# First batch of an attention and MLP kernel: inputs laid out as six tokens a row, and one order for its softmax and weight conversions

## The chip, the cores and the metric

One core of a Trainium2 chip. The metric is the device time of one execution in microseconds (us), median of several. TensorE (PE) multiplies matrices; VectorE (DVE), ScalarE (ACT) and GpSimd (POOL) work elementwise; the SP queue issues the DMA transfers.

## What is computed

Inputs q, k, v are (8 batches, 8 heads, 576 tokens, 64), phi is (8, 8, 576, 32). The first stage, cut:

```
a = exp(phi - max over tokens); a = a / sum over tokens
k_m, v_m = einsum('bhsm,bhsd->bhmd', a, k or v)         # 32 memory rows a head
attn = softmax(q @ k_m.T / 8)
x = (attn @ v_m), heads side by side: (8, 576, 512)
xn = (x - mean) / sqrt(var + 1e-6) * g_ln
x = x + relu(xn @ w_ch1) @ w_ch2                          # 512 -> 2048 -> 512
```

A second block follows (gelu, a token-mixing matrix, w_out), which the change does not touch. w_ch1 and w_ch2 come as 64-bit floats, read as pairs of 32-bit words.

## The kernel before, in words

Phase 1 (`phase1`) does attention and the first MLP for batch after batch, phase 2 the second block. Matrix products run in a split form: each operand is a high part and a low remainder, three products together.

*The first batch.* `load_phi`, `load_kv`, `load_rem` (L180 to L216) lay 512 of the 576 tokens as four consecutive tokens on each of 128 partitions, and the other 64 (REM) in tiles of their own (`prz`, `kvr`). `prep_max` and `prep_exp` (L246 to L278) take the maximum over tokens and the exponential, `prep_sum` (L280) adds up on POOL, `prep_kv` (L304) multiplies phi with keys and values into `kvp`, `prep_norm` scales to `kvn`, `prep_T` turns it to `kvT`. Queries: `load_q` and `t_q` (L363) bring five tiles of 128 tokens (the last 64) and turn them; `t_scores` (L388) forms scores `sc` in three groups of tiles (0 and 1, 2 and 3, 4), turns them (`z`), takes the maximum (L413), subtracts it (L414) and exponentiates (L415); `t_norm` (L418) divides by the sum; `t_attn` (L426) turns back and splits into `aTh`, `aTl`.

*The weights.* w_ch1 comes in four quarters (fb 0 to 3) of four 128-row blocks (`load_w1`, 4 KB rows). `to_f32` (L105) turns the 64-bit words: one ScalarE step on the upper words (L114) and two VectorE steps (L115, L116). `scale_w1` (L493) multiplies by g_ln on ScalarE (L499), `center_w1` (L501) forms column means on TensorE (`cm`, L505) and subtracts them on VectorE (L507). `make_vw` (L518) multiplies with `kvT` (`pvw`, L545), and `evict_vw` (L549) splits the result into `vw`. So the MLP's first product needs only `aT` and `vw`. w_ch2 comes in 16 blocks: `split_w2` (L558) converts each and splits it (L128 on ScalarE, L129 on POOL).

*The MLP.* `m1` (L582) forms a block `ph` (L593) with `aT` and `vw`, 256 or 320 tokens wide, in two banks by turns, and `relu` evicts it (`hh` on ScalarE L579, `hl` on VectorE L580). `m2` (L612) multiplies with `w_ch2`, three blocks later. Batch 0 goes by quarters: both token ranges with fb 0 (256 wide, then 320), then both with fb 1, and so on.

*What sets the order.* Every step is an event with a written-out time (`at_time`); events run in order of time and give instructions their priority, and a planner then places them on each engine's queue by when it expects their inputs. `tc.issue_after(x)` keeps an instruction behind x in that order. All loads go out on one queue (SP). Raw weights and several other tiles share a pool of 19 buffers (`wpool`), so a load can wait for a buffer.

Of the kernel before, what the change touches and what calls it, by code (L numbers as in the profile page):

```python
# [28 lines left out]
def fused_kernel(ctx: ExitStack, tc: tile.TileContext, q, k, v, phi, g1, w1, w2, w_in, g2, w_sg, b_sg, w_out, out):  # L29
# [45 lines left out]
    es_mlp, es_w2, es_attn, es_right, es_left = ExitStack(), ExitStack(), ExitStack(), ExitStack(), ExitStack()  # L75
# [28 lines left out]

    def to_f32(raw, gate=None):  # L105

        words = raw.bitcast(U32).rearrange("p (n two) -> p n two", two=2)
        lo, hi = words[:, :, 0], words[:, :, 1]

        gates = ExitStack()  # L110
        for ins in gate or ():
            gates.enter_context(tc.issue_after(ins.ins))
        with gates:
            A.activation(hi.bitcast(F32), hi.bitcast(F32), AF.Prelu, scale=2.0 ** -112, alpha=-(2.0 ** 32))  # L114
            V.tensor_scalar(lo, lo, 29, None, op0=ALU.logical_shift_right)  # L115
            V.scalar_tensor_tensor(out=lo, in0=hi, scalar=3, in1=lo, op0=ALU.logical_shift_left, op1=ALU.bitwise_or)  # L116
        return lo.bitcast(F32)

    def split(raws, wp, scale=None, gate=None):
# [3 lines left out]
        for i, raw in enumerate(raws):  # L123
# [3 lines left out]
            if scale is None:  # L127
                A.copy(h, w)  # L128
# [16 lines left out]
    def phase1():  # L145
# [8 lines left out]
        tail = pool(es_w2, "tail", 1)  # L154
# [8 lines left out]
        st = {"lays": [], "ps0": 0}  # L163

# [14 lines left out]

        def load_phi(b, gs):  # L180
# [47 lines left out]
        def load_q(u, b, i):  # L228
            n = u["n"]
            if b == 0:  # L230
                if i % 2 == 0:
                    t = wpool.tile([P, 2, DM], F32, tag="w", name="q0") if i == 4 else tail.tile([P, 2, DM], F32, tag="vw", name="q0", bufs=VTAIL)
                    st["q0"] = t[:, 0, :], t[:, 1, :]
                t = st["q0"][i % 2].rearrange("p (c o d) -> p c o d", c=4, o=2)[:n]
                load(t.rearrange("p c o d -> p (c o) d"), q[b, :, i * P:i * P + n, :].rearrange("h p d -> p h d"))
# [68 lines left out]
        def prep_kv(b, gs):  # L304
# [3 lines left out]
            lands = [n for t in (*(t for g in gs for t in ts[g]), st["kvr", b]) for n in t[1]] if b else []  # L308
# [16 lines left out]
            for g in gs:  # L325
                if b == 0:
                    st["kvp", g] = kvps[:, g]
                else:
                    prep_norm(b, g, kvps[:, g])

        def prep_norm(b, g, kvp=None):
# [3 lines left out]
            V.tensor_scalar(kvn[:, :, g, :], st["kvp", g] if kvp is None else kvp, rs[:, g:g + 1], None, op0=ALU.mult)  # L335

        def prep_vb(b):
            kvn = st["kvn", b]
            VBh, VBl = VBs[b % 2]
            with tc.issue_after(st["kvT", b][1].ins):  # L340
# [7 lines left out]
        def prep_T(b):  # L348
# [5 lines left out]
            st["kvT", b] = kvT, A.copy(kvT, pt)  # L354
# [8 lines left out]
        def t_q(gr, i):  # L363
# [9 lines left out]
            if b == 0:  # L373
                pt = ps_0([P, 4, n], "ptq")
                for c in range(4):
                    PE.transpose(pt[:, c, :], t[:, c].rearrange("p o d -> p (o d)"), ident[:n, :n])
                A.copy(out, pt)
# [10 lines left out]
        def t_scores(gr):  # L388
# [5 lines left out]
            sc = [ps_of(b, [P, w], "sc") for _ in range(2)]  # L394
            claims = [V.memset(t[:, 0:2], 0.0).ins.name for t in sc] if b else []
            with whole(b):
                for kT, cs in parts:
                    for j in range(4):
                        for g in range(2):
                            rs_, ms = slice(64 * g, 64 * g + 64), slice(32 * j, 32 * j + 32)  # L400
                            mm = PE.matmul(sc[g][ms, cs], kT[rs_, ms], qT[rs_, j, cs], start=True, stop=True, skip_group_check=True)
                            for name in claims:
                                tc.add_manual_dep(mm.ins, name, ORDER, reason="all eight parts of the array together")
            nb = 2 * w // 32
# [4 lines left out]
            for g in range(2):  # L409
                V.transpose(out=z[:, g * w:(g + 1) * w], in_=sc[g])  # L410
# [713 lines left out]
```

## Time and profile before

| | us |
|---|---|
| three runs | 1202.42, 1204.23, 1206.3 |
| median | 1204.23 |
| the profiled execution | 1205.68 |
| its span | 1203.5 |

Over the span TensorE is busy 97%, VectorE 57%, ScalarE 39%, POOL 33%, and the mean granted clock is 0.988. In the lines below, times count from the span's start; a bracket at the end of an instruction's line is the time its engine stood idle before it and what ended that. [...]

### The profile page before, as it was taken

The numbers are of one execution on the slowest core, as the hardware profiler recorded it, in microseconds if no ns is written. First come the engines' busy times: TensorE is split into PE (matmuls) and PEld (weight loads), VectorE is DVE, ScalarE is ACT, GpSimd is POOL, SyncE is SP. The second block draws the span as 40 slices with busy tenths as digits, with TensorE's granted clock in tenths as the row PEclk, the third lists the DMA queues.
The fourth block names the chain that finished last, engine by engine and source line by source line (L and its number), as shares of the span: only waits on it lengthen the run. The fifth ranks groups of instructions, "written<-read, shape, count | busy, mean of one in ns | idle before, by whom it ended". The sixth has DMA issues, their size and how long they took to land.

```text
span 1203.5 us, 20688 instructions
## 1 busy us (share of the span) xinstructions
PE 1170.4 (97%) x7711; PEld 993.1 (83%) x7711; DVE 688.0 (57%) x1669; ACT 467.7 (39%) x1071; POOL 401.8 (33%) x622
## 2 busy tenths in 40 slices
PE   4899899999999999999999999999999999999998
PEld 3486678788788888788888888889989988998997
DVE  4886665755644645644546445567476377447532
ACT  3665332323332322422333445445444354344430
POOL 2234112311201211201211112456666475566641
PEclk9799899999999999999999999999999999999999
DMA  8984834463341543231410343032240052022201
GB/s 248 354 242 120 236 80 126 93 194 76 97 117 31 146 124 67 92 108 25 126 35 27 108 125 116 27 82 88 82 139 18 19 150 69 2 84 84 79 19 71
DMA packets 198900, 124.14 MB, mean 103 GB/s; under 512 B 93072, under 2 KB 174096, under 8 KB 198800
## 3 DMA queue, kind: packets, MB, share of 16 engines
q1 hardware_dynamic: 198800, 122.82, 35.4%
q8 instruction: 61, 1.00, 0.3%
q14 instruction: 39, 0.32, 0.1%
HBM read 99.72 MB, written 31.33 MB: 109 GB/s over the span
## 4 chain that ended last, share of the span: by engine, by line
PE 88%; DVE 6%; DMA 2%; SPq 1%; ACT 1%; issue 1%; POOL 1%; POOLq 0%; ACTq 0%; DVEq 0%
PE ph L593 16%; PE py L623 10%; PE py L625 10%; PE py L624 10%; PE pvs L1029 9%; PE po L1052 8%; PE pv L920 8%; PE pu L1004 7%; PE pvw L545 3%; DMA q<-q_d 1%; PE kvp L315 1%; SPq L87 1%; PE cm L505 1%; PE px L460 1%; DVE qT L379 1%; PE px L459 1%
## 5 line engine op out<-in xcount | busy, mean ns | idle before, releaser
L593 PE MATMUL ph<-aTh,vw 128*128 128x320 f32 (+1 forms) x1024 | 248.4, 301 | 1.4 <-ACT vw L551 1.4
L623 PE MATMUL py<-whl,hh 128*128 128x512 f32 x512 | 202.3, 397 | 6.7 <-ACT hh L579 6.5
L624 PE MATMUL py<-whl,hh 128*128 128x512 f32 x512 | 201.2, 393 | 0.0
L593 PEld LDWEIGHTS ph<-aTh,vw 128*128 128x128 f32 x1024 | 179.5, 191 | 26.0 <-issue 8.8
L625 PE MATMUL py<-whl,hl 128*128 128x512 f32 x512 | 182.7, 397 | 0.0
L579 ACT ACTIVATE hh<-ph 128x256 fp32r<-128x256 f32 x256 | 96.5, 386 | 168.5 <-PE ph L593 111.0
L580 DVE SCALAR_TENSOR_TENSOR hl<-ph,hh 128x256 fp32r<-128x256 f32 x256 | 106.4, 421 | 91.1 <-ACT hh L579 90.6
L593 PE MATMUL ph<-aTl,vw 128*128 128x256 f32 (+1 forms) x512 | 152.7, 299 | 0.0
L623 PEld LDWEIGHTS py<-whl,hh 128*128 128x128 f32 x512 | 96.5, 189 | 30.1 <-ACT hh L579 8.6
L1029 PE MATMUL pvs<-wsh,vhl 128*128 128x288 f32 x576 | 121.1, 295 | 0.0
L624 PEld LDWEIGHTS py<-whl,hh 128*128 128x128 f32 x512 | 96.7, 189 | 19.0 <-issue 0.5
L1004 PE MATMUL pu<-yTh,whl 128*128 128x288 f32 x512 | 111.0, 296 | 0.2 <-DVE ug L909 0.2
L593 PEld LDWEIGHTS ph<-aTl,vw 128*128 128x128 f32 x512 | 97.7, 191 | 11.2 <-issue 3.6
L625 PEld LDWEIGHTS py<-whl,hl 128*128 128x128 f32 x512 | 90.3, 190 | 11.9 <-issue 2.3
L1029 PEld LDWEIGHTS pvs<-wsh,vhl 128*128 128x128 f32 x576 | 94.4, 189 | 0.7
L920 PE MATMUL pv<-whl,yTh 128*128 128x512 f32 x288 | 91.0, 396 | 0.0
L1052 PE MATMUL po<-whl,gh 128*128 128x512 f32 x288 | 90.1, 391 | 0.0
L1004 PEld LDWEIGHTS pu<-yTh,whl 128*128 128x128 f32 x512 | 85.4, 189 | 1.9 <-DVE ug L909 0.9
L579 ACT ACTIVATE cr<-ph 128x64 fp32r<-128x64 f32 x128 | 28.7, 226 | 126.3 <-PE ph L593 125.7
L1032 POOL TENSOR_TENSOR gt<-gt,ug 128x288 f32<-128x288 f32 x64 | 52.9, 827 | 68.3 <-DVE gt L1031 61.8
L1029 PE MATMUL pvs<-wsl,vhl 128*128 128x288 f32 x256 | 75.6, 295 | 0.0
L1004 PE MATMUL pu<-yTl,whl 128*128 128x288 f32 x256 | 75.5, 295 | 0.0
(154 smaller groups left out, 2164.5 us busy)
## 6 DMA issues: line engine op xcount, KB each, us to landing
raw<-in_moe_w_ch_dram SPq DMA_DIRECT2D x32, 512.0 KB, 7.8
wc<-w_d SPq DMA_DIRECT2D x28, 512.0 KB, 5.7
y_d<-x SPq DMA_DIRECT2D x36, 256.0 KB, 2.2
yt<-y_d SPq DMA_DIRECT2D x36, 256.0 KB, 2.7
yr<-y_d SPq DMA_DIRECT2D x36, 256.0 KB, 2.8
kv<-in_k_dram SPq DMA_DIRECT2D x32, 256.0 KB, 3.9
kv<-in_v_dram SPq DMA_DIRECT2D x32, 256.0 KB, 4.0
out_dram<-yr SPq DMA_DIRECT2D x32, 256.0 KB, 2.0
```

The costliest lines, as they stand in the source:

```text
L545: mm = PE.matmul(ps[g][ms, :], vT[rs_, ms], ws[j // 2][rs_, j % 2, :], start=True, stop=True, skip_group_check=True)
L579: high = A.activation(out_h, src, AF.Relu)
L580: return high, V.scalar_tensor_tensor(out=out_l, in0=src, scalar=0.0, in1=out_h.bitcast(F32), op0=ALU.max, op1=ALU.subtract)
L593: R["ph"] = PE.matmul(ph, w_[:, ks], x[:, g, 0:w], start=(n == 0), stop=(n == 3 * HK - 1))
L623: PE.matmul(py, hh, wh, start=start, stop=False)
L624: PE.matmul(py, hh, wl, start=False, stop=False)
L625: PE.matmul(py, hl, wh, start=False, stop=stop)
L920: PE.matmul(pv, y[:, kc, cs], w, start=(n == 0), stop=(n == 3 * KC - 1))
L1004: PE.matmul(pu, w[:, ds_], y[:, kc, cs], start=(n == 0), stop=(n == 3 * KC - 1))
L1029: PE.matmul(pvs, v_, w_, start=(n == 0), stop=(n == len(ops) - 1))
L1032: G.tensor_tensor(out=gt, in0=gt, in1=ug, op=ALU.mult)
L1052: PE.matmul(po, gg[:, dc, cs], w, start=(n == 0), stop=(n == 3 * KC - 1))
```

## The change

For the first batch alone, phi, keys and values are loaded as six consecutive tokens on each of 96 partitions (no leftover tiles), queries of tiles 0 to 3 as pairs of consecutive tokens on 128 partitions. Sums over tokens are matmuls with a column instead of POOL additions. These inputs lie in a pool of their own (`start`), whose memory goes to the `tail` pool afterwards. The order of loads becomes: phi, keys and values, first query pair, W1 blocks 0 and 1, second query pair, W1 blocks 2 and 3, last query tile, W2 blocks 0 to 3, then fb 1; W2 blocks 4 and 5 come ahead of fb 2. On VectorE and ScalarE the first batch's conversions and softmax steps are each kept behind the one before (`st["v"]`, `st["act"]`), W2 blocks 1 to 3 behind the softmax of the last group, and fb 1 behind these. The scores of the last group take banks of another pool. Later batches keep their steps. Cut to its core:

```diff
+    def behind(gate):
+        es = ExitStack()
+        for ins in gate or ():
+            es.enter_context(tc.issue_after(ins.ins))
+        return es
...
+        def load_first(g):
+            load(st["phi", 0][:P0, 4 * g:4 * g + 4], phi[0, g].rearrange("h (p c) m -> p h c m", c=C0))
+        def load_kv0(g, n):
+            t = start.tile([P, 2, 2, C0, D], F32, name=f"kv0{g}{n}")
+            for i, src in enumerate((k, v)):
+                load(t[:P0, i], src[0, g, 2 * n:2 * n + 2].rearrange("h (p c) d -> p h c d", c=C0))
...
+        def kv_first(g):
+            for c in range(C0):
+                PE.matmul(st["sums"][:, g:g + 1], w, mcol[:P0], start=(c == 0), stop=(c == C0 - 1), skip_group_check=True)
+            for c in range(C0):
+                for j in range(4):
+                    PE.matmul(
+                        st["kvp", 0][32 * j:32 * j + 32, g],
+                        ex[:, c, j, :],
+                        st["kv0", g, j // 2][:P0, :, j % 2, c, :],
...
+        def norm_first():
+            with behind([R["word"]]):
+                V.tensor_scalar(rs, st["sums"], float(DM), 1e-9, op0=ALU.mult, op1=ALU.add)
...
         def t_q(gr, i):
...
-                    PE.transpose(pt[:, c, :], t[:, c].rearrange("p o d -> p (o d)"), ident[:n, :n])
+                            for o in range(2):
+                                PE.matmul(pt[64 * o:64 * o + 64, c, :], t[:, 2 * c + o], ident, start=True, stop=True, skip_group_check=True)
...
+        def scale_w1(fb, part=range(KC)):
...
+                    w = to_f32(raws[fb][j], [st["hl"], R["word"]] if "hl" in st else [first_grs[2]["ah"], st["v"], R["word"]])
...
         def split_w2(c):
...
-            gate = st.get("hl", tiles[1 if c == 0 else 3]["tr"])
-            W2[c] = split([raws.pop(("w2", c))], wpool, gate=[gate])
+            W2[c] = split([raws.pop(("w2", c))], wpool, gate=[st["hl"]] if c > 3 else [st["v"], st["act"]])
+            if c < 4:
+                st["v"], st["act"] = R["word"], R["high"]
...
-                        at_time(-27, load_q, us[i], ub, qi)
-                        at_time(-21 + 0.1 * tt, t_q, gr, i)
+                        at_time((-27, -26.7, -26.5)[gi], load_q, us[i], ub, qi)
+                        at_time((-20, -18.04, -17.5)[gi] + 0.01 * i, t_q, gr, i)
...
-                    at_time(-17 + 0.1 * tt, t_scores, gr)
-                    at_time(-16 + 0.1 * tt, t_norm, gr)
-                    at_time(-16 + 0.1 * tt, t_attn, gr)
+                    at_time((-18.05, -17.93, -16.35)[gi], t_scores, gr)
+                    at_time((-18.0, -17.92, -16.34)[gi], t_soft, gr)
+                    at_time((-17.3, -16.3, -16.1)[gi], t_norm, gr)
+                    at_time((-17.2, -16.2, -16.0)[gi], t_attn, gr)
...
+            if fb == 0:
+                at_time(-26.8, load_w1, 0, [0, 1])
+                at_time(-26.6, load_w1, 0, [2, 3])
+                for j in range(KC):
+                    at_time((-20.2, -19.5, -18.08, -18.02)[j], pre_w1, j)
+                    at_time((-20.1, -19.0, -18.07, -17.95)[j], word_w1, j)
+                    at_time((-18.09, -18.06, -18.01, -17.94)[j], scale_w1, 0, [j])
+            else:
+                at_time((-25.7, -2.5, 2.0)[fb - 1], load_w1, fb, range(KC))
+                at_time((-5.0, 3.0, 7.5)[fb - 1], scale_w1, fb)
+            at_time((-17.9, -0.3, 3.0 + 1.6, 7.5 + 1.6)[fb], center_w1, fb)
+            at_time((-17.1, 1.3, 3.0 + 2.8, 7.5 + 2.8)[fb], make_vw, 0, [fb])
...
-            split_at = 4.5 * (c // 4) + 0.5625 * (c % 4) - 0.6 if c > 3 else 0.9 * c - 4
-            at_time(split_at - 5 if c > 3 else -12.7 if c == 3 else 0.2 * c - 26.4, load_w2, c)
+            split_at = 4.5 * (c // 4) + 0.5625 * (c % 4) - 0.6 if c > 3 else (-17.0, -15.9, -15.8, -15.7)[c]
+            at_time(split_at - 5 if c > 5 else 0.1 * c - 3.2 if c > 3 else 0.2 * c - 26.4, load_w2, c)
```

`pre_w1` is the ScalarE step of `to_f32`, `word_w1` its two VectorE steps, `t_soft` the part of `t_scores` from the turning of the scores on.

## Rows read from the trace of the kernel before

**Rows 1.** Busy time by stretch: PE, PEld, DVE, ACT, POOL, clock, DMA share, GB/s.
```profile
0.00:13.00 13.00, 2.33 (x9) 1.39 (x9) 5.09 (x11) 1.98 (x3) 2.88 (x13) 1.00 0.70 196
13.00:24.00 11.00, 9.88 (x136) 6.84 (x136) 1.72 (x7) 4.91 (x13) 4.89 (x9) 1.00 0.96 247
24.00:41.50 17.50, 11.16 (x40) 3.03 (x40) 16.91 (x35) 12.63 (x22) 2.37 (x2) 0.62 1.01 394
41.50:58.00 16.50, 14.33 (x55) 10.85 (x56) 14.58 (x31) 10.58 (x21) 4.19 (x4) 0.78 0.85 308
62.00:90.00 28.00, 28.00 (x151) 23.41 (x151) 24.41 (x59) 16.65 (x37) 9.21 (x14) 1.00 0.80 232
90.00:100.00 10.00, 7.55 (x54) 5.51 (x53) 7.26 (x17) 8.26 (x19) 2.82 (x2) 1.00 0.49 139
140.00:1203.50 1063.50, 1054.72 (x6937) 910.78 (x6936) 593.09 (x1448) 394.47 (x918) 360.99 (x562) 1.00 0.31 86
```

**Rows 2.** Chain of waits in order of time, 0 to 62 us: start, us, what.
```profile
17.61 0.62 SPq L87
...
18.28 5.87 DMA raw<-in_moe_w_ch_dram
...
37.86 3.13 PE pvw L545 x16
```

**Rows 3.** Timeline of the SP queue: start, us, transfer, count.
```profile
0.72 1.00 SPq L87 DMA_DIRECT2D phi<-in_phi_dram  x2
...
4.10 2.36 SPq L87 DMA_DIRECT2D prz<-in_phi_dram  x2
...
11.43 6.14 SPq L87 DMA_DIRECT2D q<-in_q_dram  x5
...
18.28 9.13 SPq L87 DMA_DIRECT2D raw<-in_moe_w_ch_dram  x11
```

**Rows 4.** Timeline of all engines, 0 to 70 us.
```profile
3.63 1.94 DVE L252 TENSOR_REDUCE pm<-phi 128x128 f32<-128x512 f32 x2 [3.63 <-DMA phi<-in_phi_dram]
...
15.12 1.93 PE L315 MATMUL kvp<-kv,phi 128*32 128x128 f32 x32
...
24.18 0.43 DVE L115 TENSOR_SCALAR raw<-raw 128x512 uint32<-128x512 uint32 x1 [3.77 <-DMA raw<-in_moe_w_ch_dram]
24.52 0.77 DVE L410 STREAM_TRANSPOSE z<-sc 128x256 f32<-128x256 f32 x2
...
28.33 0.70 ACT L114 ACTIVATE raw<-raw 128x512 f32<-128x512 f32 x1 [0.58 <-DMA raw<-in_moe_w_ch_dram]
...
36.60 2.34 DVE L507 TENSOR_TENSOR wc<-wc,cm 128x1024 f32<-128x1024 f32 x2
...
41.61 0.58 PE L593 MATMUL ph<-aTh,vw 128*128 128x256 f32 x1 [0.69 <-ACT vw L551]
...
47.72 0.42 DVE L580 SCALAR_TENSOR_TENSOR hl<-ph,hh 128x256 fp32r<-128x256 f32 x1
...
61.74 1.08 ACT L551 CAST vw<-pvw 128x512 fp32r<-128x512 f32 x2 [0.47 <-PE pvw L545]
...
69.77 0.28 PE L593 MATMUL ph<-aTh,vw 128*128 128x256 f32 x1
```

**Rows 5.** Groups of instructions by shape, 0 to 62 us: count, busy, mean ns, idle before.
```profile
L114 ACT ACTIVATE raw<-raw 128x512 f32<-128x512 f32 x19 | 12.4, 676 | 3.2 <-DMA raw<-in_moe_w_ch_dram 3.1
L505 PE MATMUL cm<-wc,mcol 128*128 128x512 f32 x16 | 11.4, 852 | 4.2 <-ACT wc L499 2.4 <-DVE z L410 1.8
L116 DVE SCALAR_TENSOR_TENSOR raw<-raw 128x512 uint32<-128x512 uint32 x12 | 7.7, 673 | 0.0
L499 ACT ACTIVATE wc<-raw,g1c 128x512 f32<-128x512 f32 x8 | 5.9, 764 | 0.8 <-DVE raw L116 0.7
...
L128 ACT CAST whl<-raw 128x512 fp32r<-128x512 f32 x4 | 2.6, 681 | 1.9 <-DVE raw L116 1.9
...
L413 DVE TENSOR_REDUCE m<-z 128x16 f32<-128x512 f32 x2 | 1.3, 660 | 0.0
```

More of the change, by code (lines that the diff above doesn't have):

```diff
@@ L40, in fused_kernel @@
     KC = DM // P
+    C0 = 6
+    P0 = S // C0
     NPAIR = B // 2
@@ L180, in load_phi @@
+        def norm_first():
+            rs = at.tile([P, 2], F32, tag="rs", name="rs")
+            with behind([R["word"]]):
+                V.tensor_scalar(rs, st["sums"], float(DM), 1e-9, op0=ALU.mult, op1=ALU.add)
+            V.reciprocal(out=rs, in_=rs)
+            st["rs", 0] = rs
+            for g in range(2):
+                prep_norm(0, g, st["kvp", 0][:, g])
         def load_phi(b, gs):
@@ L408, in t_scores @@
                 z = at.tile([P, 4 * P], F32, tag="z", name="z")[:, 0:2 * w]
-            for g in range(2):
-                V.transpose(out=z[:, g * w:(g + 1) * w], in_=sc[g])
+            with behind([st["v"]] if b == 0 else None):
+                for g in range(2):
+                    V.transpose(out=z[:, g * w:(g + 1) * w], in_=sc[g])
             z3 = z.rearrange("p (b m) -> p b m", m=NM)
@@ L420, in t_norm @@
             r = at.tile([P, 16], F32, tag="r0", name="r0")[:, 0:nb]
-            V.tensor_reduce(out=r, in_=z3, axis=AX.X, op=ALU.add)
+            with behind([st["v"]] if gr["b"] == 0 else None):
+                V.tensor_reduce(out=r, in_=z3, axis=AX.X, op=ALU.add)
             V.tensor_scalar(r, r, 1e-9, None, op0=ALU.add)
@@ L504, in center_w1 @@
             for j in range(KC):
-                PE.matmul(cm, mean, ws[j // 2][:, j % 2, :], start=(j == 0), stop=(j == KC - 1))
-            for n in range(2):
-                V.tensor_tensor(out=ws[n], in0=ws[n], in1=cm.unsqueeze(1).to_broadcast([P, 2, DM]), op=ALU.subtract)
+                with behind([first_grs[1]["sc"][0]] if fb == 0 else None):
+                    PE.matmul(cm, mean, ws[j // 2][:, j % 2, :], start=(j == 0), stop=(j == KC - 1))
+            with behind([st["v"]] if fb == 0 else None):
+                for n in range(2):
+                    ins = V.tensor_tensor(out=ws[n], in0=ws[n], in1=cm.unsqueeze(1).to_broadcast([P, 2, DM]), op=ALU.subtract)
+            if fb == 0:
+                st["v"] = ins
         def store_w1(fb):
@@ L549, in evict_vw @@
         def evict_vw(b, turn):
-            for ps, (h, l) in zip(st.pop(("vw", b, turn)), VW[b, TURNS[b % 2][turn]]):
-                A.copy(h, ps)
-                V.tensor_tensor(out=l, in0=ps, in1=h.bitcast(F32), op=ALU.subtract)
+            with behind([st["v"], st["act"]] if b + turn == 0 else None):
+                for ps, (h, l) in zip(st.pop(("vw", b, turn)), VW[b, TURNS[b % 2][turn]]):
+                    high = A.copy(h, ps)
+                    low = V.tensor_tensor(out=l, in0=ps, in1=h.bitcast(F32), op=ALU.subtract)
+            if b + turn == 0:
+                st["v"], st["act"] = low, high
         def load_w2(c):
```

215 lines of the change are left out of this document (146 added, 69 removed).

## The prediction

> **What bounds the kernel now.** I read the busy time by stretch first. From 140 us to the end TensorE is busy 1054.72 of 1063.5 us at full clock, and from 62 to 90 us all of 28 [rows 1]: after 62 us the kernel is TensorE's work, and nothing the change touches makes that work less. What can be had lies ahead of 62 us. [...] So the question is how many us earlier batch 0's MLP starts, and whether the lead is kept up to where TensorE stays full.
>
> The chain of waits through these 62 us comes second. Up to 18 us it is the SP queue issuing loads; then 5.87 us for the first W1 row block to land; later the wait for pvw, 3.13 us [rows 2]. The SP queue's own timeline says why: 22 issues, for the inputs and g1c, precede W1, two of them 2.36 us on 32-row leftovers, five 6.14 us on queries, and the first raw goes out at 18.28 [rows 3]. On the engines' timeline VectorE stands still 3.77 us until that block lands at 24.18, the fourth W1 block holds ScalarE until 28.33, centring W1 ends at 36.60 + 2.34 = 38.94, and the first MLP matmul starts at 41.61 [rows 4]. From 24 to 41.5 VectorE is busy 16.91 of 17.5 [rows 1], with W1's words and the softmax mixed. So the start is bound by loads up to 28.33, then by VectorE.
>
> **The loads.** Shapes give 0.59 MB of phi and 2.36 MB of keys and values. Runs of 512 bytes become 768 (phi) and 1536 (keys, values), and the 128- and 256-byte leftovers go. Queries go from 256-byte to 512-byte runs, 0.52 MB a pair. Rates per full DMA share: 196/0.70 = 280 GB/s in the stretch of mostly 512-byte runs, 394/1.01 = 390 in that of 4 KB runs [rows 1]. No row shows 768 or 1536 bytes; 280 and 390 are the ends, and I take the middle, 340. The first 0.26 MB of phi has landed at 3.63 [rows 4]; at 280 that is 0.9 us of moving, so the stream starts at 2.7. Then phi, keys and values end at 2.7 + 2.95/0.34 = 11.4, the first pair of query tiles at 13.3, W1 blocks 0 and 1 (0.52 MB each, 1.34 us) at 14.6 and 16.0, the second query pair at 17.9, blocks 2 and 3 at 19.2 and 20.5. Issuing doesn't hold this: 12 issues instead of 22 go ahead of W1, at some 0.5 us each [rows 3], so it is issued near 7 us, behind bytes still in the queue. Block 3 lands 7.8 us earlier than now; with 280 for the inputs it is 22.3, with 390 19.4. Behind W1 the queue now has four W2 blocks, then the next W1 quarter (fb 1); its last block lands 8 x 1.34 us later, near 31.
>
> **Small edits costed at nothing.** Six tokens a row mean 96 instead of 80 phi-by-kv matmuls, and queries turn with eight two-pass matmuls a tile instead of four transposes. The row has 32 such instructions in 1.93 us, 0.06 each [rows 4]: 1 us and some 2 us more, plus twelve column sums. What hides them is the wait for W1 up to 20.5; without that cover it is 3 to 5 us on the front chain. The POOL sums and the leftovers' maxima go, under the same cover. The scaled W1 tiles now take memory over from the first batch's inputs, whose last readers are done before W1's block 2 lands: no wait. W2's low halves on POOL come earlier, at a POOL busy 4.19 of 16.5 us [rows 1]: nothing.
>
> **From block 3 to the first MLP matmul.** The new order puts VectorE at: word 2, softmax of group 0, word 3, softmax of group 1, centring. A word is 0.42 + 0.67 us [rows 4, 5]. A group's softmax front is 0.77 for two turns [rows 4], 0.66 for the maximum and about as much for the subtraction, which has its shape [rows 5]: 2.1. Block 2 lands at 19.2; its ScalarE step 0.68 and second word step 0.67 end at 20.6; group 0 ends at 22.7, word 3 at 23.8, group 1 at 25.9. Block 3 is scaled 0.76 later, at 24.6. The eight cm passes start after group 1's scores, near 22. [...] Centring (2.34) therefore ends between 28.2 and 31.1; I take 30.5, since the low clock filled this stretch before. On VectorE the weights of group 0 (two 0.66 operations and two short ones, 1.7 as an estimate) and their turn (0.7) follow, then on ScalarE their copy and that of vw, 0.7 each as other 512-wide copies [rows 5]; pvw itself runs beside: first MLP matmul at 34.3 where it was 41.61. **Term 1: 7.3 us earlier**, with ends of 4.9 (inputs at 280 and centring at 31.1, 2.4 later) and 10.7 (390 and 28.2, 3.4 earlier).
>
> **From there to 62 us.** Now the stall is VectorE's backlog: the first hl is evicted only at 47.72 [rows 4], and its bank keeps the third MLP block from TensorE. The same backlog (softmax of group 2, weights of groups 1 and 2, W2's first word, 6 us) stands behind the earlier start, so I move this stall along and credit nothing.
>
> What is late next is fb 1's weights. Before, its four ScalarE steps ran ahead of need; now the order has W2 blocks 1 to 3 and then fb 1 behind group 2, and on ScalarE each W2 step goes behind the last one's copy. One loop is step 0.68, word 0.67, copy 0.68 or scaling 0.76 [rows 5], 2.1 us, seven in line. Group 2 is done near 42.3; seven loops end at 57, last cm pass and centring at 60, pvw and its copy at 62.4. Who waits behind them: the evictions of MLP blocks on ScalarE and VectorE, and then TensorE. Before, fb 1's copy ran at 61.74, yet its first user, the first 128x256 block of the second quarter, starts at 69.77 [rows 4]: 8 us of slack. Moved by 7.3 this user is due at 62.5. So the slack is just used up. If the evictions of eight blocks also stand in those loops (0.4 to 0.6 each), it is up to 67, 4.5 us given back; if they fit the third of the time in which ScalarE is idle (10.58 of 16.5 busy [rows 1]), none. **Term 2: 1.3 us given back**, ends 0 and 4.5.
>
> **Sum.** 7.3 - 1.3 = 6.0 us. The profiled execution took 1205.68 us, of which 1203.5 is the span: it would take 1199.7. It stood 1.45 us above the median of 1204.23, so for the median I predict 1198.2. After 62 us I add nothing: TensorE is full to 90 us with the DMA engines at 0.80 of their time, and 90 to 100 us keeps its 2.45 idle [rows 1].
>
> **Rivals.** (a) *Loads on 96 partitions are slower.* If the rate goes with the partitions filled, it is 3/4 of 390 = 293 GB/s: 10.1 us for 2.95 MB, 1.4 later, 1199.6. For: no row has such a load; against: the same engines reach 280 with much shorter runs [rows 1].
> [...]
>
> (b) *The stall up to 50 us goes as well.* The stretch 41.5 to 58 has 14.33 us busy at 0.78, so some 5.3 of 16.5 are lost [rows 1]. If the fixed order lets hl through early and the clock stays up, 4 of those come on top: about 1194. Against: VectorE's list is not shorter.
>
> (c) *Given back.* The seven loops hold fb 1 to 67 us and more, or the front gains only its 4.9: less than 3.6 us stay, 1201 to 1204. What speaks for it: fb 1's slack goes to zero in my own sum.
>
> (d) *Slower.* One mechanism: TensorE runs out at the border of the first quarter because fb 1 is behind all of W2 0 to 3. It decides once fb 1's vw comes after 69.8; at 3.7 us a loop instead of 2.1 (each waiting in line for an eviction that waits for TensorE) it is 62.4 + 7 x 1.6 = 73.6, and the time 1208. Against it: ScalarE's idle third.
>
> (e) *The change doesn't do what it says:* the planner still sends W1 behind the queries, or word 2 holds the softmax as long as raws did. That is no change, and lies in (c).
>
> **Chances.** A difference of 0.3%, 3.6 us, is about the least that a measurement of this kernel tells from none. Forecast (1195 to 1200.5) 0.46, (a) 0.13, (b) 0.13: faster 0.72. (c) and (e) 0.16: within 0.3%. (d) 0.12: slower. The range takes in forecast, (a), most of (b) and (c): 1191.5 to 1205.
>
> **What would show it.** Right: the first raw issued near 7 us, block 3 landed near 20.5, no leftover loads; centring of fb 0 ending at 28 to 32; the first MLP matmul at 32 to 36; the first 128x256 block of the second quarter near 64; from 90 us on, everything moved by the same 6 us. Wrong: phi, keys and values at under 280 GB/s; VectorE idle ahead of word 2 or 3 with scores ready; TensorE idle before the second quarter, with ScalarE waiting on words of W2 or fb 1; more than 2.5 us idle at the later stall near 85 to 95 us.

## The result: 1% slower, and the profile after

The changed kernel takes 1216.06 us (median of 6 runs, 1211.87 to 1217.37), the kernel before 1203.92 beside it: a ratio of 1.0096, interval 1.0078 to 1.0115. The profiled execution of the changed kernel has a span of 1214.5 us, 11.0 more than before.

Busy time by stretch of the changed kernel first: the stretches of [rows 1], then four narrower ones (columns as in [rows 1], the clock as a share of full speed).

```profile
0.00:13.00 13.00, 4.29 (x16) 3.36 (x16) 5.61 (x8) 2.97 (x3) 2.87 (x13) 1.00 0.90 228
13.00:24.00 11.00, 11.00 (x134) 9.84 (x135) 2.39 (x7) 0.92 (x2) 0.00 (x0) 1.00 1.09 363
24.00:41.50 17.50, 11.97 (x126) 5.78 (x122) 12.06 (x21) 9.77 (x19) 0.82 (x1) 1.00 0.82 320
41.50:58.00 16.50, 12.22 (x51) 9.43 (x50) 12.82 (x33) 9.77 (x23) 4.13 (x4) 0.73 0.64 200
62.00:90.00 28.00, 24.23 (x117) 17.67 (x116) 22.48 (x45) 20.65 (x38) 8.67 (x12) 0.88 0.90 265
90.00:100.00 10.00, 10.00 (x63) 7.77 (x62) 7.67 (x23) 3.51 (x10) 1.54 (x5) 1.00 0.59 181
140.00:1203.50 1063.50, 1056.97 (x6978) 911.43 (x6977) 598.40 (x1461) 397.91 (x928) 363.50 (x566) 1.00 0.31 86
...
5.00:10.00 5.00, 2.29 (x6) 1.37 (x6) 4.53 (x8) 0.00 (x0) 0.00 (x0) 1.00 1.07 278
10.00:15.00 5.00, 4.00 (x40) 3.86 (x44) 0.94 (x2) 1.69 (x2) 0.00 (x0) 1.00 1.13 284
15.00:20.00 5.00, 5.00 (x60) 4.45 (x56) 1.78 (x5) 0.68 (x1) 0.00 (x0) 1.00 1.07 396
...
41.10:77.60 36.50, 28.41 (x127) 20.54 (x127) 30.56 (x65) 25.85 (x53) 11.62 (x11) 0.84 0.79 252
```

TensorE is now full from 13 to 24 us, VectorE stands almost idle there (2.39 of 11), and from 24 to 41.5 VectorE is busy 12.06 us where it was 16.91. From 62 to 90 us TensorE, full before, loses 3.8 us and part of its clock (0.88 granted). From 140 us on TensorE is idle 6.5 us in all, no more than the 8.8 of before: most of the damage is done ahead.

The timeline shows where. First what answers to [rows 4], with some rows between.

```profile
11.01 2.72 PE L237 MATMUL sums<-mcol,ex 96*128 96x1 f32 x12 [1.23 <-ACT ex L228]
13.65 2.79 PE L240 MATMUL kvp<-kv,ex 96*32 96x128 f32 x48
...
17.10 0.68 ACT L119 ACTIVATE raw<-raw 128x512 f32<-128x512 f32 x1 [5.28 <-DMA raw<-in_moe_w_ch_dram]
...
21.73 3.59 PE L460 MATMUL ptq<-ident,q 128*64 128x128 f32 x32
...
25.25 0.44 PE L430 MATMUL ptk<-ident,kvn 128*128 128x128 f32 x2
...
26.42 0.36 ACT L433 COPY kvT<-ptk 128x256 f32<-128x256 f32 x1
...
26.55 0.69 DVE L124 SCALAR_TENSOR_TENSOR raw<-raw 128x512 uint32<-128x512 uint32 x1 [4.07 <-ACT raw L119]
...
28.70 0.77 DVE L507 STREAM_TRANSPOSE z<-sc 128x256 f32<-128x256 f32 x2
...
35.03 1.22 DVE L630 TENSOR_TENSOR wc<-wc,cm 128x1024 f32<-128x1024 f32 x1 [0.84 <-PE cm L627]
...
41.14 0.51 PE L722 MATMUL ph<-aTh,vw 128*128 128x256 f32 x2 [2.63 <-ACT vw L677]
...
50.48 0.30 ACT L542 CAST aTh<-z 128x128 fp32r<-128x128 f32 x1 [1.76 <-DVE z L530]
...
54.31 1.30 POOL L143 TENSOR_TENSOR whl<-raw,whl 128x512 fp32r<-128x512 f32 x1 [8.68 <-ACT whl L142]
...
54.85 1.31 DVE L124 SCALAR_TENSOR_TENSOR raw<-raw 128x512 uint32<-128x512 uint32 x1 [0.90 <-ACT raw L119]
...
75.57 1.33 PE L670 MATMUL pvw<-wc,kvT 64*32 64x512 f32 x16 [3.10 <-DVE pvw L661]
...
76.93 1.07 ACT L677 CAST vw<-pvw 128x512 fp32r<-128x512 f32 x2 [0.76 <-PE pvw L670]
...
77.57 0.58 PE L722 MATMUL ph<-aTh,vw 128*128 128x256 f32 x1 [0.67 <-ACT vw L677]
```

W1's first block is there at 17.10 in place of 24.18. But the first MLP matmul starts at 41.14 where it was 41.61, and the second quarter's first block at 77.57 where it was 69.77 [rows 4]. So two things happened. Ahead of the first MLP matmul the lead vanished: TensorE works without a break from 11.01 to 25.69 on column sums (L237), kvp (L240) and query turns (L460), the keys' copy (L433) comes at 26.42, and VectorE waits 4.07 us for ScalarE's step on W1 block 1, which stands in line behind two query copies. And the first quarter of the MLP takes 36.4 us instead of 28.2. What TensorE waits for in it (waits of PE, 41.1 to 77.6 us: us in total, times, longest):

```profile
PE ph L722 <- ACT vw L677: 3.3, 2, 2.6
PE pvw L670 <- DVE pvw L661: 3.1, 1, 3.1
PE ph L722 <- ACT aTh L542: 2.5, 1, 2.5
PE py L752 <- ACT whl L142: 1.1, 1, 1.1
```

The SP queue did as the change says: no leftovers, W1 issued from 9.46 us, in place of 18.28 [rows 3].

```profile
9.46 3.31 SPq L89 DMA_DIRECT2D raw<-in_moe_w_ch_dram  x2
...
16.56 7.94 SPq L89 DMA_DIRECT2D raw<-in_moe_w_ch_dram  x8
```

The groups by shape (0 to 26 us for the first three, 0 to 75.5 for the last two: count, busy, mean ns, idle before) have the terms of the sum. The means of PE rows overlap (96 kvp rows of 420 ns are busy 5.6 us in all); a row of the timeline divided by its count is the better price.

```profile
L240 PE MATMUL kvp<-kv,ex 96*32 96x128 f32 x96 | 5.6, 420 | 0.0
L237 PE MATMUL sums<-mcol,ex 96*128 96x1 f32 x24 | 5.4, 354 | 1.2 <-ACT ex L228 1.2
L460 PE MATMUL ptq<-ident,q 128*64 128x128 f32 x32 | 3.6, 419 | 0.0
...
L124 DVE SCALAR_TENSOR_TENSOR raw<-raw 128x512 uint32<-128x512 uint32 x18 | 14.8, 830 | 6.7 <-ACT raw L119 6.3
L123 DVE TENSOR_SCALAR raw<-raw 128x512 uint32<-128x512 uint32 x18 | 8.9, 497 | 6.2 <-DMA raw<-in_moe_w_ch_dram 6.2
```

### The profile page after: what moved, and what is told of

Its sections match the earlier page's. It is cut to its first block, busy times and chain, and to the rows that moved or that the text cites. A ratio compares the mean times of both kernels' runs of the same rounds, so it can differ in the third digit from the quotient of the medians.

```text
span 1214.5 us, 20838 instructions
## 1 busy us (share of the span) xinstructions
PE 1179.4 (97%) x7797; PEld 1002.7 (83%) x7797; DVE 694.6 (57%) x1664; ACT 467.8 (39%) x1069; POOL 398.4 (33%) x617
## 4 chain that ended last, share of the span: by engine, by line
PE 85%; DVE 7%; DMA 4%; ACT 1%; issue 1%; SPq 1%; POOL 1%; DVEq 0%; POOLq 0%
PE ph L722 16%; PE py L752 10%; PE py L753 10%; PE py L754 10%; PE pvs L1174 8%; PE po L1197 8%; PE pv L1065 8%; PE pu L1149 7%; PE pvw L670 2%; DVE raw L124 1%; PE kvp L396 1%; DMA q<-q_d 1%; SPq L89 1%; DVE raw L123 1%; PE cm L627 1%
## 5 line engine op out<-in xcount | busy, mean ns | idle before, releaser
L1174 PE MATMUL pvs<-wsl,vhl 128*128 128x288 f32 x256 | 75.6, 295 | 0.0
L1149 PE MATMUL pu<-yTl,whl 128*128 128x288 f32 x256 | 75.5, 295 | 0.0
```

The source lines that it names most:

```text
L1149: PE.matmul(pu, w[:, ds_], y[:, kc, cs], start=(n == 0), stop=(n == 3 * KC - 1))
L1174: PE.matmul(pvs, v_, w_, start=(n == 0), stop=(n == len(ops) - 1))
```

## The experiments

All marks in one table, each from the run's timeline (us): start of the keys' copy, of the first MLP matmul, of group 2's weight copy, of pvw of the second quarter (fb 1), and of the second quarter's first 128x256 block; then the ratio to the kernel before, with its interval. Differences between runs are read from the ratios.

| run | keys | first MLP | group 2 | pvw fb 1 | 2nd quarter | ratio |
|---|---|---|---|---|---|---|
| before | 21.0 | 41.6 | 46.7 | 60.6 | 69.8 | 1 |
| after | 26.4 | 41.1 | 50.5 | 75.6 | 77.6 | 1.0096 [1.0078, 1.0115] |
| e1_free | 28.9 | 45.7 | 61.9 | 72.0 | 76.1 | 1.0084 [1.0063, 1.0104] |
| e2_sums | 21.4 | 36.1 | 46.4 | 71.3 | 75.9 | 1.0057 [1.0041, 1.0074] |
| e3_qold | 23.8 | 38.1 | 47.4 | 72.3 | 76.9 | 1.0076 [1.0056, 1.0096] |
| e4_serial | 20.9 | 40.3 | 43.2 | 66.0 | 69.0 | 0.9998 [0.9987, 1.0008] |
| e5_front | 22.8 | 38.0 | 48.9 | 73.7 | 76.1 | 1.0057 [1.0042, 1.0072] |
| e7_loose | 25.5 | 40.2 | 50.5 | 75.1 | 79.0 | 1.0090 [1.0072, 1.0108] |
| e8_vb | 24.5 | 40.1 | 51.2 | 75.6 | 77.5 | 1.0094 [1.0069, 1.0118] |
| e9_all | 24.4 | 40.0 | 50.4 | 74.1 | 78.0 | 1.0066 [1.0044, 1.0089] |
| x1_last | 25.7 | 40.4 | 51.1 | 73.6 | 76.9 | 1.0132 [1.0115, 1.0149] |
| x3_noorder | 33.4 | 49.5 | 59.2 | 67.7 | 75.7 | 1.0075 [1.0060, 1.0090] |
| x6_noorder_sums | 30.6 | 46.7 | 50.2 | 62.9 | 78.5 | 1.0096 [1.0081, 1.0111] |
| x5_w1first | 28.0 | 46.4 | 48.6 | 61.3 | 76.9 | 1.0023 [1.0012, 1.0034] |
| y2_early | 26.0 | 40.9 | 51.3 | 71.6 | 76.0 | 1.0060 [1.0045, 1.0075] |
| y1_early_sums | 23.3 | 38.2 | 47.6 | 67.5 | 73.1 | 1.0041 [1.0027, 1.0056] |
| y4_last | 21.8 | 36.7 | 47.0 | 70.5 | 74.4 | 1.0025 [1.0012, 1.0039] |
| z1_late | 21.3 | 41.4 | 53.8 | 61.7 | 69.6 | 1.0010 [1.0000, 1.0019] |
| z2_early | 22.4 | 40.6 | 50.6 | 59.3 | 68.4 | 0.9969 [0.9957, 0.9981] |

**First set: parts of the change, and one part put into the kernel before.** e1_free gives W2 0 to 3 and fb 1 their gates and times of before:

```diff
-W2[c] = split(..., gate=[st["hl"]] if c > 3 else [st["v"], st["act"]])
+W2[c] = split(..., gate=[st.get("hl", first_grs[0 if c == 0 else 1]["tr"])])
```


> The changed kernel, with the conversions of W2 blocks 0 to 3 and of fb 1 given back the places and gates they had before (behind group 0 and group 1 only, W2 by turns with fb 1); loads, layouts and the order up to the first MLP matmul stay. Theory A (the loss is TensorE standing idle before the second quarter, because fb 1 is converted behind group 2 and W2): the second quarter's first block, at 77.6 us in the changed kernel and 69.8 before, comes back to 68 to 71, and the time to 1204 to 1208. Rival B (the loss is the front: matmuls of sums and query turns fill TensorE from 13.7 to 25.3 us and delay kvT to 26.4): the first MLP matmul stays at 41 and the time stays above 1212.

e2_sums takes the column sums off TensorE:

```diff
-for c in range(C0): PE.matmul(st["sums"][:, g:g+1], ex[:, c], mcol[:P0], ...)
+V.tensor_reduce(out=sm, in_=ex.rearrange("p c h m -> p (h m) c"), axis=AX.X, op=ALU.add)
+PE.matmul(st["sums"][:, g:g+1], sm, mcol[:P0], ...)
```


> The changed kernel, with the twelve column-sum matmuls of a group (2.72 us of TensorE) replaced by one VectorE reduction over the six tokens (1.4 us, on an engine that idles there) and one matmul. Theory A: kvT comes up to 4 us earlier than 26.4, and as everything behind it is one chain, the time falls by 2 to 4 us, to 1212 to 1214, still above the kernel before. Rival B: the whole loss is here; the time falls by 5 us and more.

e3_qold loads and turns the queries as before (`PE.transpose` of a 128-token tile, four a tile).

> The changed kernel, with the queries of tiles 0 to 3 loaded and turned as before: 256-byte runs, one 128x128 transpose for two heads instead of two-pass matmuls against the identity for each head. TensorE's 32 matmuls of a pair (3.59 us, 0.11 each) become 8 transposes (some 1 us); the loads take some 0.5 us longer a pair. Theory A: kvT some 2 us earlier, the time 1 to 3 us lower, 1213 to 1215. Rival B: 4 us lower and more. If runs of 512 bytes are worth more than the turns cost, the time rises.

e4_serial is the kernel before with the changed kernel's line for W2 1 to 3 and fb 1, each behind the last and all behind group 2:

```diff
-gate = st.get("hl", tiles[1 if c == 0 else 3]["tr"])
+gate = ... [tiles[TB]["tr"], tiles[TB]["ah"]] if c == 1 else [R["word"], R["high"]]
```


> The kernel before, with the one part of the change that theory A blames: W2 blocks 1 to 3 converted behind the softmax of group 2, each behind the last one's copy, and fb 1 behind these (W2 blocks 0 to 3 all loaded ahead, as in the change). Theory A: the second quarter's first block goes from 69.8 to 76 to 79 us and the time to 1210 to 1215. Rival B: within 2 us of the kernel before.

Taking the sums off TensorE gives the keys' copy at 21.4 and the first MLP matmul at 36.1: 5 us each, and 0.4% of the time (4.7 us, between what A and B had said). The queries give 0.2%, within the intervals. Freeing the conversions let the first steps on W2's blocks 0 to 2, which wait for their loads (ScalarE stands idle 7.46 us for the first, up to 24.80), stand ahead of the query copies and the keys, and the front got later by 4.6 us; neither A nor B had that. And e4_serial costs nothing in the kernel before, as B said: pvw is 5.4 us later there, but the 8 us of slack of [rows 4] swallow it. So the fixed line alone is not the loss. What is striking is e2_sums: TensorE starts the MLP 5.5 us before the kernel before does and the second quarter 6.1 us after it.

**Second set: does the front add up, and is it the line?**

e5_front is e2_sums with e3_qold; e7_loose lifts "each behind the last" (all stay behind group 2; first pair of lines); e8_vb (second pair) puts the copies of the values' low and high halves right behind the keys' copy; e9_all is all of these.

```diff
-w = to_f32(raws[fb][j], ... [first_grs[2]["ah"], st["v"], R["word"]])
+w = to_f32(raws[fb][j], ... [first_grs[2]["ah"], first_grs[2]["lo"]])
...
-with behind([st["act"] if b == 0 else st["kvT", b][1]]):
+with behind([st["kvT", b][1]]):
```


> The changed kernel, with both reliefs of TensorE together: sums by one VectorE reduction and one matmul a group, queries loaded and turned as before. Theory C (one chain: the front up to kvT, then the softmax of all groups, then W2 blocks 1 to 3 and fb 1 in line, 25 us from the copy of group 2's weights to pvw of fb 1; the kernel before with the same line lost nothing since its group 2 was done at 43.2 instead of 50.5): kvT at 18 to 20, group 2 at 43 to 45, pvw of fb 1 at 68 to 70, second quarter's first block at 71 to 74, time 1206 to 1210. Rival D (what is left after 50 us does not depend on when the front ends, since raws and buffers of W2 and fb 1 set it): the second quarter stays at 75 to 77 and the time at 1210 to 1212.

> The changed kernel, with W2 blocks 1 to 3 and fb 1 still behind group 2, but no longer each behind the last one's word and copy. Theory C: the 25 us from group 2's copy (50.5) to pvw of fb 1 fall to some 15 to 18, pvw at 66 to 69, the second quarter at 69 to 72, time 1206 to 1210. Rival D: pvw at 73 and more, time above 1212.

> The changed kernel, with the copies of the values (VBh, ScalarE, four of 0.3 us) behind kvT as before, at some 27 us, instead of behind W2 block 3's copy at 59.4. Products with VBh can then fill TensorE's waits between 45 and 65 us. Theory C: they take 3.6 us out of the work after the second quarter's start at most, and the chain to pvw of fb 1 stays at 75; time 1213 to 1216. Rival E (TensorE lacks filler work, not fb 1): second quarter no earlier, but the first y store 3 us earlier, time 1211 to 1213.

> All three together: front relief, loose order of W2 and fb 1, early VBh, on the changed kernel's loads. Theory C: kvT at 18 to 20, pvw of fb 1 at 58 to 62, second quarter at 62 to 66, time 1198 to 1203, below the kernel before. Rival D: second quarter at 70 and more, time 1204 to 1210.

None gains on e2_sums. Theory C missed its marks in e5_front, e7_loose and e9_all; rival D's came out in e5_front (76.1 and 1211.6) and e7_loose (75.1 and more than 1212). e8_vb comes to 1216.9, near what C has for it. With the conversions behind group 2, pvw of fb 1 comes 22.8 us after group 2's weights in e4_serial and 23.7 to 25.1 in these four, e2_sums, e3_qold and after; in the kernel before it is 13.9.

**Third set: the order off, six word steps back, and W1 first without the change.** x1_last holds the word steps of fb 2 and W2 4, 5 behind fb 1's centring. x3_noorder drops every gate of the first batch and takes the times of before; x6_noorder_sums adds e2_sums. x5_w1first is the kernel before with one number changed, W1 ahead of the queries in the load queue.

```diff
-w = to_f32(raws[fb][j], [st["hl"], R["word"]] if "hl" in st else ...
+w = to_f32(raws[fb][j], [st["hl"], R["word"], st["c", fb - 1]] if "hl" in st else ...
...
-at_time((-26.5, -26.2, -2.5, 2.0)[fb], load_w1, fb)
+at_time((-27.1, -26.2, -2.5, 2.0)[fb], load_w1, fb)
```


> The changed kernel, with the conversions of the third quarter of W1 and of W2 blocks 4 and 5 held behind the centring of W1's second quarter in the planner's line, as they stood before the change. The changed kernel has 18 pairs of word steps (8.9 and 14.8 us) on VectorE ahead of the second quarter's vw, the kernel before 12 (4.5 and 7.7 us): 11.5 us more, of which some 4 are a stretch of each step and some 7 are the six more pairs. Theory E (those six pairs are what delays the second quarter's W1): pvw of the second quarter near 68 in place of 75.57, the second quarter's first 128x256 block near 71 in place of 77.57, and 5 to 7 us less: near 1210. Rival F (VectorE's count isn't the limit; the second quarter's W1 stands behind W2 0 to 3 in a chain that goes through ScalarE and POOL): pvw stays at 74 to 76 and the time within 2 us of 1216.

> The changed kernel with its layouts and its order of loads, but without the one written order: the planner puts the first batch's softmax, centring, W1 and W2 conversions and the copies for the keys where the kernel before let it, with the times of before. Theory G (the order is what loses, the layouts gain what they should): the first MLP matmul near 37 to 39, the softmax weights of groups 1 and 2 done before 46, the second quarter's first block near 68 and the time near 1202. Rival H (TensorE's work for the sums and the query turns, in front of the keys, is what loses): the keys' copy still at 26, the first MLP matmul at 41 or later, the second quarter's first block at 73 to 76 and the time 1208 to 1214.

> As the run without the written order, and the twelve column sum matmuls replaced by one reduction on VectorE and one matmul a group. Theory G with H (two causes, sums and order, that add): the keys' copy near 21.5, the first MLP matmul near 35, the second quarter's first block near 65 and the time 1197 to 1200, which is what was predicted for the change. Rival (what is gained ahead of the first MLP matmul is lost up to the second quarter, whatever the order, as in the runs with the front relieved): the second quarter's first block at 70 or later and the time 1204 or more.

> The kernel before with one edit: W1's first four blocks are issued ahead of the five query loads. W1's first block was issued at 18.28 and landed by 24.18, its fourth by 28.33; six us of issue earlier gives the fourth block near 22, the queries some 2.5 us of issue later (transfers of W1 ahead of them, some 6 us). Theory (waiting for W1 to 28.33 is what set the first MLP matmul): centring 4 to 6 us before 36.6, first MLP matmul 36 to 38, time 1199 to 1201. Rival (the queries' softmax takes the place of W1 as the last thing, or VectorE is full from 24 anyway): centring 35 or later, time within 2 us of 1204.

In all four the theory missed, and in three the rival's marks came out in part: x6_noorder_sums has the second quarter at 78.5 and 1215.5 us, where its rival has 70 or later and 1204 or more; x3_noorder comes to 75.7 and inside rival H's times, though not with its keys; and in x5_w1first the centring starts at 41.4, where the rival has 35 or later. Without six pairs of word steps pvw came only 2 us earlier, and the third quarter paid for it (it starts at 107.1 us, in after at 103.2): theory E falls. Without the order ScalarE puts first steps that wait for W2's loads ahead of the query copies, the keys come at 33.4, and the MLP starts 8 us late; that this loses no more than the change does shows how little the start alone decides. x5_w1first is not the clean trial of an early W1 that it was meant to be, since the keys came 7 us late with the queries.

**Fourth set: the conversions' first steps in ScalarE's idle stretch.** Ahead of group 0's weights ScalarE waits 4.9 us for VectorE. y2_early puts there its seven first steps on W2 1 to 3 and fb 1, and the values' copy; the word steps follow group 2 in one run. y1_early_sums adds e2_sums.

```diff
+def pre_more():
+    for raw in [raws["w2", c] for c in (1, 2, 3)] + raws[1]:
+        with behind([st["act"]]):
+            st["act"] = upper(words_of(raw))
+at_time(-17.35, pre_more)
```


> The changed kernel with the column sums by one reduction on VectorE and one matmul a group, and its conversions no longer one behind the other after group 2: ScalarE's first step on W2 blocks 1 to 3 and on the second quarter of W1 stands in ScalarE's idle stretch ahead of group 0's weights (4.85 us idle there in the run with the sums moved), VBh too, and VectorE's seven pairs of word steps follow group 2's low weights in one run. Theory J (the time from group 2's weights to the second quarter's pvw, 25 us in every run that keeps the written order against 14 in the kernel before, is what takes back an early first MLP matmul): group 2's weights at 46, the seven pairs done by 54, pvw of the second quarter at 60 to 63, the second quarter's first block at 64 to 67 and 1199 to 1203. Rival K (the second quarter's start is bound elsewhere, since six runs came to 75 to 79 whatever was moved): first block at 74 or later, 1209 or more.

> The same placing of the conversions, but with the twelve column sum matmuls of the changed kernel: the keys' copy at 26 and the first MLP matmul at 41 as there. Theory J: group 2's weights near 50.5, pvw of the second quarter at 64 to 67, the second quarter's first block at 68 to 71 and 1204 to 1209; the difference to the other run of this call is what the sums cost, 4 to 5 us. Rival K: first block at 75 or later and within 3 us of 1216.

From group 2's weights to pvw it is now 20.3 and 19.9 us, some 5 less, but not the 14 of before. 0.36% and 0.55% of the 0.96% are back; of the second, e2_sums alone has 0.39%, and its interval overlaps that of y1_early_sums. Both runs miss the marks of theory J, and the second quarter of y2_early, at 76.0, is where rival K has it, in a time that K has not. So a shorter way from group 2 to pvw may be worth something; that it is the cause of the loss is not shown. On the engines' timeline of y1_early_sums the rest of the stretch shows:

```profile
51.94 5.01 POOL L144 TENSOR_TENSOR whl<-raw,whl 128x512 fp32r<-128x512 f32 x3 [9.19 <-ACT whl L143]
...
52.41 5.69 DVE L124 SCALAR_TENSOR_TENSOR raw<-raw 128x512 uint32<-128x512 uint32 x4
```

Three of the word steps take 1.66 to 1.80 us each here, beside three subtractions of 1.58 to 1.76; the fourth, after them, takes 0.68, as it does elsewhere (0.69 for DVE, 26.55 in the timeline of after). POOL's 1.30 at 54.31 there is of a subtraction that began first: the word step that began in it, at 54.85, took 1.31.

**Fifth set: is VectorE full, and who sets the second quarter?** z1_late and z2_early add reductions to the kernel before that nobody reads, in VectorE's full stretch (in t_norm of group 1) and in its idle one (in prep_T); y4_last is y1_early_sums with x1_last.

```diff
+for _ in range(3):
+    V.tensor_reduce(out=dum, in_=z3, axis=AX.X, op=ALU.add)
...
+for _ in range(5):
+    V.tensor_reduce(out=dum[:, 0:4], in_=kvn, axis=AX.X, op=ALU.add)
```


> The kernel before with three further reductions on VectorE (128x512 to 128x16, 0.66 us each, 2.0 us in all, read by nobody) beside group 1's sums, in the stretch from 24 to 41.5 where VectorE was busy 16.91 of 17.5 us. Theory L (VectorE is full there, so that the wait for W1 held back nothing that an earlier W1 could have started): the first MLP matmul 1.3 to 2 us after 41.61, the second quarter's pvw about 2 us after 60.56, and 1 to 2 us more. Rival M (the wait for W1 and ScalarE's chain set the end of this stretch, VectorE has room): first MLP matmul within 0.5 us of 41.61, time within 0.7 us of before.

> The kernel before with five further reductions on VectorE (128x256 to 128x4, some 0.42 us each, 2.1 us in all, read by nobody) right behind the keys' normalization at 20 us, where VectorE waited 3.77 us for W1's first block. Theory L: the idle stretch takes them, nothing moves, time within 0.7 us of before. If this run loses as much as the other, neither says anything of a full VectorE: the added instructions alone cost.

> The run with early first steps and the sums on VectorE (1208.81), and the word steps of the third quarter and of W2 4 and 5 held behind the centring of the second quarter, three pairs of which (3.3 us) stood ahead of it there. If the second quarter's start is still bound by its W1 (pvw at 67.49, vw awaited 1.56 us): pvw at 63 to 65, the second quarter's first block near 70 and 1205 to 1207. If TensorE's own backlog from the first quarter binds it: first block at 72 or later, 1208 or more.

z1_late: the marks of the start don't move (41.4 and 69.6), group 2's weights come 7 us later, and the time is 0.1% up, with an interval that reaches to none. So a VectorE that is 97% busy there still had room up to the second quarter, and theory L's marks fall. Its time, 1 to 2 us more, isn't told from none. z2_early is the surprise: it is 0.31% *faster* than the kernel before, the only kernel here that beats both. The 2.2 us of useless work came with another order of much that follows. On VectorE's timeline it stands here:

```profile
21.87 1.78 DVE L353 TENSOR_REDUCE dum<-kvn 128x4 f32<-128x256 f32 x4
24.05 0.43 DVE L115 TENSOR_SCALAR raw<-raw 128x512 uint32<-128x512 uint32 x1 [0.40 <-DMA raw<-in_moe_w_ch_dram]
```

Its MLP starts 1.0 us earlier, its second quarter 1.3, and the first y_d store 3.4 (143.40 for 146.76); e4_serial and z1_late have that store just as early and gain nothing by it, so the lead of z2_early is one that lasts. Which of the many moved instructions does it was not tried. It sets a limit to this study: two kernels that the planner orders anew can differ by 3 to 4 us for no reason that the edit names. The differences of 0.2% above are not read as causes.

In y4_last neither expectation came out whole: pvw is at 70.5, later than in y1_early_sums, the second quarter at 74.4, and the time, 1206.62, can't be told from that of y1_early_sums. TensorE doesn't wait for fb 1 any more at the second quarter (its waits, 36.7 to 74.4 us, in a profiled execution that took 3.4 us more than the median):

```profile
PE py L762 <- POOL whl L144: 3.1, 1, 3.1
PE ph L731 <- ACT vw L686: 2.8, 1, 2.8
PE ph L731 <- ACT aTh L544: 2.3, 1, 2.3
```

The first of these is the pair of engines again. Four word steps keep their 0.68 us, and the one subtraction that runs beside them takes 3.71 (51.72 to 55.43); the next two take 1.30 each:

```profile
51.72 6.24 POOL L144 TENSOR_TENSOR whl<-raw,whl 128x512 fp32r<-128x512 f32 x3 [10.49 <-ACT whl L143]
51.79 2.49 DVE L124 SCALAR_TENSOR_TENSOR raw<-raw 128x512 uint32<-128x512 uint32 x4
```

The same stretch, first MLP matmul to second quarter, as busy time (columns as in [rows 1]) in the kernel before:

```profile
41.60:69.80 28.20, 26.13 (x131) 20.46 (x132) 22.52 (x50) 19.03 (x39) 4.09 (x4) 0.87 0.91 319
```

in e4_serial:

```profile
40.30:69.00 28.70, 24.62 (x126) 17.55 (x126) 24.51 (x54) 21.39 (x44) 6.60 (x6) 1.00 0.98 345
```

in e2_sums:

```profile
36.10:75.90 39.80, 30.81 (x127) 22.38 (x128) 32.54 (x66) 26.52 (x55) 10.92 (x11) 0.81 0.77 244
```

and in y4_last:

```profile
36.70:74.40 37.70, 30.85 (x126) 23.12 (x127) 26.41 (x65) 19.84 (x41) 10.41 (x6) 0.77 0.75 242
```

e4_serial gives the work by itself: 24.62 us at full clock. What is busy beyond that is, as an estimate, the half clock (granted 0.50, as from 54 to 58 us in after), and the rest is idle. After: 24.6 + 3.8 + 8.1. e2_sums: 24.6 + 6.2 + 9.0. y4_last: 24.6 + 6.2 + 6.9. Before: 24.6 + 1.5 + 2.1 idle, but only roughly, since its stretch holds other matmuls (12 rows more of px, 8 fewer of py). A start 5 us earlier finds its work not ready: TensorE waits for group 0's vw, group 1 and 2's weights (46 to 51 us in after, e2_sums and y4_last, 46.7 before), W2 1 (converted near 50 to 55), and behind these waits the granted clock is down (0.73 from 41.5 to 58 us in after), which the work that is left pays. In e4_serial no gap of the stretch is longer than 1.4 us, and the clock stays at 1.00.

This stretch is not the whole account. By the start of the second quarter after is 7.8 us behind the kernel before, at the first y_d store 9.0, at a later store (215.91 before, 226.35 after) 10.4, and from there on it loses little more (11.0 in the span). Busy time up to that store, where all hold the same ph, py and px matmuls, in before, after, y4_last and z2_early:

```profile
0.00:215.91 215.91, 188.00 (x1266) 140.31 (x1267) 140.97 (x339) 97.13 (x217) 53.72 (x83) 0.94 0.66 198
0.00:226.35 226.35, 196.77 (x1352) 150.03 (x1353) 146.69 (x334) 97.56 (x215) 51.16 (x78) 0.95 0.64 189
0.00:220.40 220.40, 192.19 (x1332) 146.42 (x1332) 144.66 (x336) 96.70 (x215) 53.64 (x78) 0.95 0.66 194
0.00:212.20 212.20, 184.99 (x1266) 138.19 (x1267) 141.89 (x344) 97.49 (x217) 53.33 (x83) 0.96 0.68 201
```

After has 8.8 us more of TensorE busy and only 1.7 more idle. The work that the change adds is of that size: ahead of the first MLP matmul the sums take 5.4 us, the query turns 5.8 where they took 2.4, and kvp 5.4 where it took 4.9. Ahead of that matmul TensorE stands idle less than before (14.2 us for 18.2) and nothing runs at half clock (granted 1.00 up to 41.1 us), but the added work eats that up; the idle time comes back in the first quarter. So the first quarter's waits stand in for waits that the front had before, and what is left over is about the added work. z2_early has its lead from fewer busy us on the same matmuls, at a mean clock of 0.96 for 0.94. These are accounts and not trials: only the sums' part was taken out by itself and gave its price (e2_sums).

## Why the prediction was wrong

**Loads: right in kind, too fast.** W1 did go out ahead, at 9.46 where I had 7, and its first block landed at 17.10, not 14.6, its fourth near 23.5, not 20.5. The first loads ran at 278/1.07 = 260 and 284/1.13 = 251 GB/s per full share (5 to 15 us, mostly phi, keys and values), below my low end of 280; the stretch right behind, mostly 4 KB runs, at 396/1.07 = 370. Rival (a), for which the rate goes with the partitions filled, came nearest: three quarters of 370 is 278, and the two rates lie within a tenth of that. But runs of 768 and 1536 bytes come together with the 96 partitions, and no run here parts them: why these loads were slower is not shown.

**"Small edits costed at nothing" failed first.** I priced sums, kvp and query turns at 0.06 us each, 3 to 5 us, covered by the wait for W1. The timeline has 2.72/12 = 0.23 a row of column sums (each of the twelve calls is two rows), 2.79/48 = 0.06 a kvp and 3.59/32 = 0.11 a query turn. The sums alone are 5.4 us, ahead of the keys and not beside them, and with turns and kvp the added work is some 9 us where I had 3 to 5. And the cover was not there: TensorE works without a break up to 25.69, while W1's first two blocks lie ready from 17.1 and 18.4. e2_sums shows the price of the sums: 5.0 us of the start (36.14 for 41.14). The other 1.8 us to my 34.3 are not accounted for. In e2_sums VectorE still waits 2.24 us, up to 21.56, for ScalarE's step on W1 block 1, which stands behind two query copies though its block was there at 17.98; no run put that step first.

**Term 1 failed in size, and it counted what is not a gain.** The first MLP matmul came 0.5 us earlier where I had 7.3. No run shows the 30.5 that this sum takes for the end of centring: in after the eight cm passes run from 30.71 to 34.99 us at a granted clock of 1.00 and centring ends at 37.38, in e2_sums at 32.39. And with the start 5.5 us earlier, in e2_sums, the time is still 0.57% above before, so the 7.3 us would have been wrong as a sum even as a right date: an earlier first MLP matmul is worth something only if groups 1 and 2, W2 1 to 3 and fb 1 come earlier too. In before they were prepared while W1 was on its way and converted; the order puts them behind the centring, and group 2's weights come at 46.4 at best, as before (46.7).

**Term 2 failed in size.** I had the copy behind pvw end 20.1 us behind group 2 (42.3 to 62.4) and gave 1.3 us back. Measured are 27.2 us, from 50.78 to 78.00, and a group 2 that is 8.5 us late. Two of the loops took 2.6 us instead of 2.1: the word step stretched from 0.69 to 1.31 while POOL subtracted (54.31 and 54.85 in the timeline). Six pairs of word steps for fb 2 and W2 4, 5 stood ahead of fb 1's centring too, 18 pairs where [rows 5] has 12; I hadn't seen that the order doesn't hold these back, though x1_last, which held them back and was slower, shows no gain in that alone. The step that failed is the one that compared vw's date with a due date and took everything else as TensorE's full speed: the half clock and the idle cost 8.3 us in the first quarter, and no row of mine priced them.

**Rival (d) has the way it moved**, and its sign came out: vw of fb 1 at 76.93, after 69.8, and TensorE idle 3.10 us ahead of pvw at the border. Its chance of 0.12 was too small and its price, 1208, 8 us too low. But its mechanism is not shown to be the cause. e4_serial has the same line at no cost, e7_loose lifts it and its gain is inside the intervals, and 8.1 us are idle through the whole first quarter, not at its border alone.

**What was right:** no leftovers, W1 ahead of most of the queries, and what is lost early stays lost, but only from the store of 215.91 on: it comes at 226.35, 10.4 later, and the span is 11.0 longer. The second quarter's start does not tell the time: x5_w1first is 7.1 us late there, 0.2 at the first y_d store and 1.9 in the span.

**Open:** with sums, first steps and word steps put right (y4_last) 0.25% are left, some 3 us. That is as much as a new order by the planner makes by itself, so their cause isn't settled. Where they are lost can be said: y4_last is 1.0 us behind at the first y_d store and 4.5 at the one of 215.91 (4.7 in the span), in the account of busy time 4.2 of them as more busy time of TensorE and 0.3 as more idle. From 140 to 180 us, where batch 1 starts, TensorE is idle 5.0 us, 3.4 in the kernel before. The query turns are part of that work, but e5_front, which has them as before, gains nothing on e2_sums. Nor is it tried which rows of the fast z2_early matter.

## What to carry to other kernels

A transfer that an engine waits for is worth its wait only if nothing else was done during it: list what the waiting time was used for, and give that work its new place and price before the gain is counted. An early start of the busiest engine is worth as much as its second and third inputs are early; with gaps behind it, it also paid in clock here (0.84 granted from 41.1 to 77.6 us in after, 1.00 from 40.3 to 69.0 in e4_serial). And when a planner orders the line, put one neutral edit beside the trial: here five useless reductions gained 0.31%, 2 to 5 us by the interval.

## What the runs showed of the hardware that was not expected

A matmul with one moving column costs 0.23 us a row here, four times a 128-column kvp at 0.06 (both f32, both 96 rows of input): what differs is the weights (96*128 against 96*32 by their tiles), and the weight loads are busy 9.84 of 11 us in that stretch; that the price is theirs was not tried alone. VectorE's two-input word step and POOL's subtraction held each other up here, and not evenly. In y1_early_sums their ends alternate, 0.55 and 1.16 us apart, with 1.66 to 1.80 a word step and 1.58 to 1.76 a subtraction; in y4_last the word steps keep 0.68 and one subtraction takes 3.71; apart they take 0.68 and 1.30. The half clock in the first quarter cost between 0 us (e4_serial, granted clock 1.00) and, as an estimate, 6.2 (y4_last, 0.77) on as many matmuls (126 rows each).
